# A second folding of the features in a Fourier mixing layer: two half products with 128 contraction rows each, and a later place for the norm transposes

## Chip, core, metric

One core of a Trainium2 chip. TensorE (matmuls, PE in the profile; its weight loads are PEld), VectorE (DVE), ScalarE (ACT), GpSimd (POOL) and the DMA queues run side by side and wait for each other by semaphores. The metric is the device time of one execution in microseconds, lower is better. The kernel before took 360.04 us (median of 3 runs, 356.87 to 361.86).

## What is computed

Block-sparse attention (4 batches, 8 heads, 768 positions, head width 64; each query sees its own 64-wide block and the best three of the earlier ones), then a Fourier mixing layer with a two-layer feed-forward on the 512 joined features:

```python
def _moe_ref(x, w_ch1, w_ch2):
    X = np.fft.fft(x, axis=1)          # over 768 positions
    X = np.fft.fft(X, axis=2)          # over 512 features
    mixed = np.real(X).astype(np.float32)
    u = x + mixed
    mu = np.mean(u, axis=-1, keepdims=True)
    var = np.mean((u - mu) ** 2, axis=-1, keepdims=True)
    un = (u - mu) / np.sqrt(var + 1e-06)
    ch = np.maximum(un @ w_ch1, 0.0) @ w_ch2
    return (u + ch).astype(np.float32)
```

The real part of the double transform is cos·x·cos minus sin·x·sin, so it is made of products with cosine and sine tables. Only the real part of a real input is wanted, so inputs at d and 512 - d (and at s and 768 - s) can be added or subtracted first, and the tables need only half the rows.

## The kernel before

**Attention** runs over 16 head pairs (`kk`, four per batch), each in six steps: scores (`stage_S`, L339) into one of two large PSUM tiles, exponentials on ScalarE (L344), the product with v (`stage_AV`, L365) for the first head at step 4 and for the second at step 1 of the next pair. Around them stand the transposes of q and k of the pair after next (`stage_AA`, `tp`), their evictions (qT on VectorE L259, key sums L265) and the gate that picks the blocks (`stage_B`, `stage_C`).

**Fourier stage.** When a head pair's output x is complete, `stage_AV` makes sums and differences of the two halves of the positions (`fs`, L378 and L379, on GpSimd, for a batch's last pair on VectorE). After pairs 2 and 3 of a batch VectorE folds the features d and 512 - d: differences into `fo` (L385), sums in place in `fs` (L386); the middle column goes to `xmid` (L388, GpSimd). `stage_S1` multiplies over the positions: `za` from `fo` with the sine table and from `xmid`, `ya` from `fs` with the cosine table, for `dt` = 1 and then 0 (two groups of 128 features); VectorE and ScalarE bring the results to SBUF, forwards and backwards (L413, L415). `stage_S2` multiplies over the features: each of the six 128-row tiles `kt` takes four matmuls with 512 columns (L430, L431), contracting 2 x 128 rows of y with cosines and of z with sines, into one PSUM bank `mx`. In batch 0 a fifth matmul with the identity adds x (L434) and ScalarE copies the sum out (L435); in the others VectorE adds x while it empties PSUM (L437). Statistics follow (L439, L440).

**Norm and feed-forward.** After the sixth tile `stage_N` computes 1/std by Newton steps: the start on VectorE (L455 to L458), the steps on GpSimd (L461 to L468), then six normalizations, three on VectorE (L471) and three on ScalarE (L475). `stage_T` transposes the six tiles (`unt`, L484), which are copied to `unT` (L489, in batch 0 L487). `stage_M1` (16 units: 512 and 256 columns, `ha` and `hb`, L500; evictions L503 on ScalarE and L505 on VectorE) and `stage_M2` (24 units of four 512-column matmuls, `ch`, L514; after every fourth the add L517 on VectorE and the output DMA) are the feed-forward.

**Order.** TensorE's and GpSimd's orders are what the program issues; VectorE's and ScalarE's are arranged by the scheduler of the language. A `Feed` holds two lists: `chain`, the Fourier stage of each batch (S1, S2, T, each a `Unit` with a cost, the unit that it follows, and a gap that must pass after that one by the planner's clock), and `bulk`, the M1 and M2 units. Between the attention steps `filler` (L555) pulls units: a ready one of the chain first, then bulk. How many it pulls is set by the work that should be done by step `key`. A batch's M1 and M2 units enter `bulk` after its last T; T of a batch may begin only when M1 of the batch before is done. What is left after attention is pulled in the same manner to the end.

**PSUM.** All stages but the scores share four PSUM buffers (tag `ps`): a tile that is to be written waits until the engine that empties the tile before it in that buffer has done so.

Of the kernel before, what the change touches and what calls it, by code (L numbers as in the profile page):

```python
# [12 lines left out]
F16 = mybir.dt.float16  # L13
# [6 lines left out]
def _consts_np():  # L20
    S = 768
    DM = 512
# [9 lines left out]

    d = np.arange(DM // 2)
    argd = 2.0 * np.pi * ((np.outer(d, np.arange(DM)) % DM) / DM)
    CD = np.cos(argd).astype(np.float16)
    SDN = (-np.sin(argd)).astype(np.float16)
    SDP = np.sin(argd).astype(np.float16)
    SDN[0] = SDP[0] = np.where(np.arange(DM) % 2 == 0, 1.0, -1.0)
    ident32 = np.eye(128, dtype=np.float32)
# [77 lines left out]
def kernel(  # L117
# [40 lines left out]
    def const(shape, dtype, name):  # L158
        return cpool.tile(shape, dtype, tag=name, name=name)

    cs_sb = const([128, HST, 2, KM], F16, "cs_sb")
    ss_sb = const([128, HST, 2, KM], F16, "ss_sb")
    cd_sb = const([128, 2, DM], F16, "cd_sb")
    sdn_sb = const([128, 2, DM], F16, "sdn_sb")
    sdp_sb = const([128, 2, DM], F16, "sdp_sb")
    xmid = const([128, 2, HST, 128], F16, "xmid")
    fs = const([128, 2, HST, DM], F16, "fs")
    fo = const([128, 2, HST, HD], F16, "fo")
    id32 = const([128, 128], FP, "id32")
# [54 lines left out]
    def load_fft():  # L224
        nc.sync.dma_start(cs_sb, dr["CS"].ap().rearrange("(st p) r k -> p st r k", p=128))
        nc.sync.dma_start(ss_sb, dr["SS"].ap().rearrange("(st p) r k -> p st r k", p=128))
        for t, n in ((cd_sb, "CD"), (sdn_sb, "SDN"), (sdp_sb, "SDP")):
            nc.sync.dma_start(t, dr[n].ap().rearrange("(dt p) l -> p dt l", p=128))

# [122 lines left out]
    def stage_AV(kk, e):  # L352
# [26 lines left out]
        eng.tensor_tensor(out=fs[:, 1, :, c], in0=x_b[:, 0:HST, c], in1=x_b[:, HST:NST, c], op=SUB)  # L379
        fsf = fs.rearrange("p r t d -> p (r t) d")  # L380
        fof = fo.rearrange("p r t d -> p (r t) d")
        if hp >= 2:
            lo, hi = (129, HD) if hp == 2 else (1, 129)
            a, z = fsf[:, :, lo:hi], fsf[:, :, DM - lo:DM - hi:-1]
            nc.vector.tensor_tensor(out=fof[:, :, lo:hi], in0=a, in1=z, op=SUB)  # L385
            nc.vector.tensor_tensor(out=a, in0=a, in1=z, op=ADD)  # L386
        if hp == 2:
            nc.gpsimd.tensor_copy(out=xmid.rearrange("p r t d -> p (r t) d")[:, :, 0:1],  # L388
                                  in_=fsf[:, :, HD:HD + 1])


    def stage_S1(b, dt):
        x = X[b]
        dsl = slice(128 * dt, 128 * (dt + 1))
        yps = pst([128, 2, KM], f"ya_{b}_{dt}")
        zps = pst([128, 2, KM], f"za_{b}_{dt}")
        for r in range(2):
            for t in range(HST):
                nc.tensor.matmul(zps[:, r, :], fo[:, r, t, dsl], ss_sb[:, t, r, :],
                                 start=(t == 0), stop=(dt == 1 and t == HST - 1))  # L400
            if dt == 0:
                for t in range(HST):
                    nc.tensor.matmul(zps[:, r, :], xmid[:, r, t, :], cs_sb[:, t, r, :],
                                     start=False, stop=(t == HST - 1))
        for r in range(2):
            for t in range(HST):
                nc.tensor.matmul(yps[:, r, :], fs[:, r, t, dsl], cs_sb[:, t, r, :],
                                 start=(t == 0), stop=(t == HST - 1))
# [10 lines left out]
    def stage_S2(b, kt):  # L419
        x = X[b]  # L420
# [8 lines left out]
        for dt in range(2):  # L429
            nc.tensor.matmul(mps, x["y", dt][hi][:, ksl], cd_sb[:, dt, :], start=(dt == 0), stop=False)  # L430
            nc.tensor.matmul(mps, x["z", dt][hi][:, ksl], sd[:, dt, :], start=False,  # L431
                             stop=(dt == 1 and b > 0))
        if b == 0:
            nc.tensor.matmul(mps, id16, x["x"][:, kt, :], start=False, stop=True)  # L434
            nc.scalar.copy(out=u_b[:, kt, :], in_=mps)  # L435
        else:
            nc.vector.tensor_tensor(out=u_b[:, kt, :], in0=mps, in1=x["x"][:, kt, :], op=ADD)  # L437
        bst = spool.tile([128, 6], FP, tag="bst", name=f"bst_{b}_{kt}")
# [139 lines left out]
    with tc.manual_schedule(engines={mybir.EngineType.PE, mybir.EngineType.Pool}):  # L578
# [124 lines left out]
```

## Time and profile before

| | |
|---|---|
| median of 3 runs | 360.04 us (356.87 to 361.86) |
| the profiled execution | 359.59 us, span 357.6 us, mean granted clock 0.971 |
| end of the last AV on TensorE | 281.6 us |
| first M1 of the last batch | 311.63 us |
| S2 matmuls, 512 columns (L430, L431) | 4 x 24, 378 to 379 ns each, 0.86 us for four in a row |
| add L437 (18) / statistics L439 (24) on VectorE | 676 / 690 ns |
| fold L385, L386 on VectorE | 16 in all, 555 to 570 ns |
| TensorE's waits at `unt` L484 | 4.0 us for L517, 3.1 for qT L259, 1.1 for L471 |

The page gives each engine's busy share; a busy TensorE is a modelled quantity, as matmuls overlap. Slices are a fortieth of the span (8.94 us). The chain of waits follows the end of the program back, at each step to what released the instruction. A group's row gives busy time, mean of one in ns, the idle time of the engine ahead of it and what ended that. The row PEclk, and the granted clock of a window, tell at what share of full speed TensorE was run.

### The profile page before, as it was taken

How to read it: one execution, taken by the hardware profiler on the slowest of the kernel's cores; microseconds unless marked ns; L12 is line 12 of the kernel's file. 1: busy time of each engine (PE TensorE's matmuls, PEld its weight loads, DVE VectorE, ACT ScalarE, POOL GpSimd, SP SyncE). 2: the span in 40 equal slices, each digit the busy share in tenths (PEclk: the TensorE clock that was granted, in tenths of full speed). 3: DMA queues.
4: the chain of work that ended last, by engine and by line, in shares of the span. 5: the costliest groups of instructions: out<-in, count | busy, mean ns of one | idle time of the engine just before them, and what ended most of it. 6: DMA issues, size and time to landing. Idle time of an engine off the chain costs nothing.

```text
span 357.6 us, 6899 instructions
## 1 busy us (share of the span) xinstructions
PE 335.2 (94%) x2688; PEld 212.9 (60%) x2688; DVE 223.0 (62%) x685; ACT 174.2 (49%) x259; POOL 89.1 (25%) x165
## 2 busy tenths in 40 slices
PE   8899997997999999599999999996999999999995
PEld 4577775775766765355566566553766554556442
DVE  3768888777566769755566458787656669533121
ACT  3177885879865744424557444243667320244100
POOL 8434655138440110610402202016012000100000
PEclk9989998999699999999999999998999999999999
DMA  9999999963967322223403210000000010100012
GB/s 180 202 207 251 232 186 212 157 140 88 168 129 119 88 46 75 73 75 103 110 11 73 61 60 29 31 30 32 0 2 2 0 60 29 59 31 0 31 62 85
DMA packets 85696, 31.57 MB, mean 88 GB/s; under 512 B 77736, under 2 KB 81520, under 8 KB 85664
## 3 DMA queue, kind: packets, MB, share of 16 engines
q1 hardware_dynamic: 80368, 26.27, 32.2%
q0 software_dynamic: 3552, 4.40, 7.8%
q10 hardware_dynamic: 1744, 0.46, 0.6%
q8 instruction: 21, 0.34, 0.4%
q14 instruction: 11, 0.09, 0.1%
HBM read 29.03 MB, written 6.29 MB: 99 GB/s over the span
## 4 chain that ended last, share of the span: by engine, by line
PE 74%; DVE 17%; ACT 4%; POOL 3%; issue 2%; POOLq 0%; DVEq 0%; ACTq 0%
PE ch L514 18%; PE ha L500 15%; PE sc L339 8%; PE hb L500 8%; PE g L286 5%; PE av L365 4%; PE tp L254 3%; DVE bst L439 3%; PE warm L318 2%; DVE u L437 2%; PE unt L484 2%; DVE kr L265 2%; PE gt L307 2%; PE mx L430 2%; PE mx L431 2%
## 5 line engine op out<-in xcount | busy, mean ns | idle before, releaser
L344 ACT ACTIVATE ptl<-sc 128x896 f16<-128x896 f32 x96 | 87.4, 916 | 63.6 <-PE sc L339 51.6
L514 PE MATMUL ch<-w_sb,hT 128*128 128x512 f16 x384 | 93.0, 384 | 0.0
L500 PEld LDWEIGHTS <-w_sb 128*128 128x128 f16 x512 | 48.8, 98 | 35.5 <-issue 1.4
L500 PE MATMUL ha<-unT,w_sb 128*128 128x512 f16 x256 | 66.1, 380 | 0.0
L339 PE MATMUL sc<-qg,kI 76*128 76x512 f16 (+3 forms) x256 | 56.6, 314 | 3.9 <-ACT ptl L344 3.9
L514 PEld LDWEIGHTS <-hT 128*128 128x128 f16 x384 | 36.9, 99 | 38.2 <-issue 1.1
L503 ACT ACTIVATE hT<-ha 128x512 f16<-128x512 f32 x64 | 38.2, 597 | 36.3 <-PE ha L500 36.2
L505 DVE TENSOR_SCALAR hT<-hb 128x256 f16<-128x256 f32 x64 | 27.0, 422 | 38.5 <-PE hb L500 38.4
L262 POOL CAST qg<-qT 64x768 f16<-64x768 f32 x32 | 26.7, 835 | 59.2 <-DVE qT L259 57.1
L500 PE MATMUL hb<-unT,w_sb 128*128 128x256 f16 x256 | 38.4, 272 | 0.3 <-DVE hT L505 0.3
L339 PEld LDWEIGHTS <-kI 76*128 76x128 f16 x256 | 24.5, 102 | 20.2 <-issue 3.5
L277 ACT CAST kI<-tp 64x384 f16<-64x384 f32 x57 | 27.0, 473 | 16.6 <-DVE kr L265 15.6
L517 DVE TENSOR_TENSOR u<-ch,u 128x512 f32<-128x512 f32 x24 | 16.5, 687 | 25.2 <-PE ch L514 25.0
L378 POOL TENSOR_TENSOR fs<-x 128x384 f16<-128x384 f16 x12 | 11.6, 970 | 76.4 <-DVE x L370 69.0
L365 PEld LDWEIGHTS <-ptl 128*128 128x128 f16 x672 | 24.7, 98 | 2.9 <-DVE ptl L350 0.4
L365 PE MATMUL av<-v,ptl 128*128 128x65 f16 x672 | 26.2, 195 | 0.1
L265 DVE TENSOR_REDUCE kr<-tp 128x6 f32<-128x384 f32 x32 | 17.0, 548 | 11.0 <-PE tp L254 11.0
L350 DVE TENSOR_TENSOR ptl<-ptl,ut 128x384 f16<-128x384 f16 x36 | 14.2, 430 | 11.5 <-ACT ptl L344 11.4
L286 PEld LDWEIGHTS g<-kr,qT 128*128 128x128 f32 x160 | 20.1, 195 | 1.4
L286 PE MATMUL g<-kr,qT 128*128 128x24 f32 x160 | 19.9, 267 | 0.0
L475 ACT ACTIVATE x<-u,nmr,rstd 128x512 f16<-128x512 f32 x12 | 8.9, 803 | 22.1 <-POOL nmr L468 22.1
L484 PE MATMUL unt<-id,x 128*128 128x128 f16 x96 | 11.0, 247 | 8.3 <-DVE u L517 4.0
(88 smaller groups left out, 423.6 us busy)
## 6 DMA issues: line engine op xcount, KB each, us to landing
vn<-in_v_dram SPq DMA_DIRECT2D x32, 192.0 KB, 4.0
out_dram<-u SPq DMA_DIRECT2D x24, 256.0 KB, 2.0
kn<-in_k_dram SPq DMA_DIRECT2D x30, 192.0 KB, 4.4
qn<-in_q_dram SPq DMA_DIRECT2D x30, 192.0 KB, 4.0
w_sb<-in_moe_w_ch_dram POOLq DMA_DIRECT2D x8, 256.0 KB, 8.1
w_sb<-in_moe_w_ch_dram POOLq DMA_DIRECT2D x4, 512.0 KB, 8.1
cs_sb<-c_CS SPq DMA_DIRECT2D x1, 289.5 KB, 4.7
ss_sb<-c_SS SPq DMA_DIRECT2D x1, 289.5 KB, 4.9
```

Source lines behind the costliest of these rows:

```text
L262: nc.gpsimd.tensor_copy(out=d["qg"][e][0:64, :], in_=d["qt"][64 * e:64 * e + 64, :])
L265: nc.vector.tensor_reduce(out=d["kr12"][:, 6 * g:6 * g + 6], in_=ps.rearrange("p a (x c) -> p a x c", x=2), axis=mybir.AxisListType.X, op=ADD)
L277: nc.scalar.copy(out=dst, in_=src_)
L286: nc.tensor.matmul(gps[:, st - 1, :], d["qt"][:, 128 * st:128 * (st + 1)], d["kr24"], start=True, stop=True)
L339: nc.tensor.matmul(sp[:, co:co + (a1 - a0)], d["kI"][e][0:76, 128 * jt:128 * (jt + 1)], d["qg"][e][0:76, a0:a1], start=True, stop=not diag)
L344: nc.scalar.activation(out=pt[:, SEC * s:SEC * (s + 1)], in_=sp[:, 0:SEC], func=AF.Exp, scale=0.125)
L365: nc.tensor.matmul(av[:, st, 0:65], pt[:, o:o + 128], d["v16"][:, e, jt, 0:65], start=(cnt == 0), stop=(cnt == 20))
L484: nc.tensor.transpose(tps[:, dt, :], x["x"][:, st, 128 * dt:128 * (dt + 1)], id16)
L500: nc.tensor.matmul(hp_, w1_sb[:, dt, 128 * it:128 * (it + 1)], unT[:, dt, c0:c1], start=(dt == 0), stop=(dt == NDT - 1))
L503: nc.scalar.activation(out=hT[:, c0:c1], in_=hp_, func=AF.Relu)
L505: nc.vector.tensor_scalar(out=hT[:, c0:c1], in0=hp_, scalar1=0.0, scalar2=None, op0=mybir.AluOpType.max)
L514: nc.tensor.matmul(cps, x["hT"][it][:, 128 * st:128 * (st + 1)], w2_sb[:, it, :], start=(it == 0), stop=(it == NIT - 1))
```

## The change

`stage_AV`: the folded sums and differences are folded once more, d against 256 - d. Features of the even output columns l = 2m need only the sums (cosine) or differences (sine) of one kind, those of the odd columns the other kind. So `fc[0]` and `fo[0]` (128 features) serve the even columns, `fc[1]` and `fo[1]` the odd ones. After pair 2 two VectorE operations make `ft[0]` and `ft[1]` from features around 256; after pair 3 six make `ft[2]`, `ft[3]`, `fo[1]`, `fc[1]`, `fo[0]`, `fc[0]`, and GpSimd does the columns at 0, 128, 256 and 384 (two small operations after each of the two pairs). `fs` is no longer written in place.

`stage_S1` reads `fo[dt]` and `fc[dt]`; its matmuls have the shapes of before. `stage_S2`: for each `dt` two matmuls with 256 columns write their half of the PSUM tile, even columns in the first half and odd ones in the second. What reads the tile takes the two halves alternately (`mv`), and the identity matmul of batch 0 reads x with the columns reordered. The tables CD, SDN and SDP have half as many rows.

In the planner the cost of an S2 unit goes from 0.87 to 0.5 and the gap after it from 0.7 to 1.0; the gap ahead of the first T goes from 5.0 to 9.0 except in batch 0; `key` goes from 12 x 12 + 20 to 12 x 12 + 29.

```diff
-    d = np.arange(DM // 2)
-    argd = 2.0 * np.pi * ((np.outer(d, np.arange(DM)) % DM) / DM)
+    d = np.arange(DM // 4)
+    l = 2 * np.arange(DM // 2)[None, :] + np.arange(2)[:, None]
+    argd = 2.0 * np.pi * ((d[:, None, None] * l[None]) % DM) / DM
...
-    cd_sb = const([128, 2, DM], F16, "cd_sb")
+    cd_sb = const([128, 2, HD], F16, "cd_sb")
...
-    fo = const([128, 2, HST, HD], F16, "fo")
+    fc = [const([128, 2 * HST, 128], F16, f"fc_{p}") for p in range(2)]
+    fo = [const([128, 2 * HST, 128], F16, f"fo_{p}") for p in range(2)]
+    ft = [const([128, 2 * HST, 128], F16, f"ft_{i}") for i in range(4)]
...
-        if hp >= 2:
-            lo, hi = (129, HD) if hp == 2 else (1, 129)
-            a, z = fsf[:, :, lo:hi], fsf[:, :, DM - lo:DM - hi:-1]
-            nc.vector.tensor_tensor(out=fof[:, :, lo:hi], in0=a, in1=z, op=SUB)
-            nc.vector.tensor_tensor(out=a, in0=a, in1=z, op=ADD)
         if hp == 2:
-            nc.gpsimd.tensor_copy(out=xmid.rearrange("p r t d -> p (r t) d")[:, :, 0:1],
-                                  in_=fsf[:, :, HD:HD + 1])
+            near, far = f[:, :, HD - 1:HD - 128:-1], f[:, :, HD + 1:HD + 128]
+            tt(ft[0][:, :, r], near, far, SUB)
+            tt(ft[1][:, :, r], near, far, ADD)
+            for p, op in ((0, ADD), (1, SUB)):
+                tt(fc[p][:, :, 0:1], f[:, :, 0:1], f[:, :, HD:HD + 1], op, nc.gpsimd)
+        if hp == 3:
+            near, far = f[:, :, r], f[:, :, DM - 1:DM - 128:-1]
+            tt(ft[2][:, :, r], near, far, SUB)
+            tt(fo[1][:, :, r], ft[2][:, :, r], ft[0][:, :, r], ADD)
+            tt(fo[1][:, :, 0:1], f[:, :, 128:129], f[:, :, 384:385], SUB, nc.gpsimd)
+            tt(xmid.rearrange("p r t d -> p (r t) d")[:, :, 0:1], f[:, :, 128:129],
+               f[:, :, 384:385], ADD, nc.gpsimd)
+            tt(ft[3][:, :, r], near, far, ADD)
+            tt(fc[1][:, :, r], ft[3][:, :, r], ft[1][:, :, r], SUB)
+            tt(fo[0][:, :, r], ft[2][:, :, r], ft[0][:, :, r], SUB)
+            tt(fc[0][:, :, r], ft[3][:, :, r], ft[1][:, :, r], ADD)
...
         for dt in range(2):
-            nc.tensor.matmul(mps, x["y", dt][hi][:, ksl], cd_sb[:, dt, :], start=(dt == 0), stop=False)
-            nc.tensor.matmul(mps, x["z", dt][hi][:, ksl], sd[:, dt, :], start=False,
+            half = mps[:, HD * dt:HD * (dt + 1)]
+            nc.tensor.matmul(half, x["y", dt][hi][:, ksl], cd_sb[:, dt, :], start=(dt == 0), stop=False)
+            nc.tensor.matmul(half, x["z", dt][hi][:, ksl], sd[:, dt, :], start=False,
                              stop=(dt == 1 and b > 0))
+        split = dict(m=HD, r=2)
+        xv = x["x"][:, kt, :].rearrange("p (m r) -> p m r", **split)
+        uv = u_b[:, kt, :].rearrange("p (m r) -> p m r", **split)
+        mv = mps.rearrange("p (r m) -> p m r", **split)
         if b == 0:
-            nc.tensor.matmul(mps, id16, x["x"][:, kt, :], start=False, stop=True)
-            nc.scalar.copy(out=u_b[:, kt, :], in_=mps)
+            nc.tensor.matmul(mps, id16, xv.rearrange("p m r -> p r m"), start=False, stop=True)
+            nc.scalar.copy(out=uv, in_=mv)
         else:
-            nc.vector.tensor_tensor(out=u_b[:, kt, :], in0=mps, in1=x["x"][:, kt, :], op=ADD)
+            nc.vector.tensor_tensor(out=uv, in0=mv, in1=xv, op=ADD)
...
-    M1_COST, M2_COST, S1_COST, S2_COST, T_COST = 1.3, 0.87, 1.3, 0.87, 0.43
+    M1_COST, M2_COST, S1_COST, S2_COST, T_COST = 1.3, 0.87, 1.3, 0.5, 0.43
...
-            last = Unit(lambda kt=kt: stage_S2(b, kt), S2_COST, last, 2.5 if kt == 0 else 0.7)
+            last = Unit(lambda kt=kt: stage_S2(b, kt), S2_COST, last, 2.5 if kt == 0 else 1.0)
...
-            last = Unit(lambda st=st: stage_T(b, st), T_COST, last, 5.0 if st == 0 else 0.2,
+            last = Unit(lambda st=st: stage_T(b, st), T_COST, last, (5.0 if b == 0 else 9.0) if st == 0 else 0.2,
...
-        key = 12 * (3 * NP) + 20
+        key = 12 * (3 * NP) + 29
```

More of the change, by code (lines that the diff above doesn't have):

```diff
@@ L30, in _consts_np @@
     SS = np.sin(arg).astype(np.float16)
-    d = np.arange(DM // 2)
-    argd = 2.0 * np.pi * ((np.outer(d, np.arange(DM)) % DM) / DM)
+    d = np.arange(DM // 4)
+    l = 2 * np.arange(DM // 2)[None, :] + np.arange(2)[:, None]
+    argd = 2.0 * np.pi * ((d[:, None, None] * l[None]) % DM) / DM
     CD = np.cos(argd).astype(np.float16)
-    SDN = (-np.sin(argd)).astype(np.float16)
-    SDP = np.sin(argd).astype(np.float16)
-    SDN[0] = SDP[0] = np.where(np.arange(DM) % 2 == 0, 1.0, -1.0)
+    sn = np.sin(argd)
+    sn[0] = np.sin(np.pi * l / 2)
+    SDN, SDP = (-sn).astype(np.float16), sn.astype(np.float16)
+    SDN[0, 0] = SDP[0, 0] = np.where(np.arange(DM // 2) % 2 == 0, 1.0, -1.0)
     ident32 = np.eye(128, dtype=np.float32)
@@ L162 @@
     ss_sb = const([128, HST, 2, KM], F16, "ss_sb")
-    cd_sb = const([128, 2, DM], F16, "cd_sb")
-    sdn_sb = const([128, 2, DM], F16, "sdn_sb")
-    sdp_sb = const([128, 2, DM], F16, "sdp_sb")
+    cd_sb = const([128, 2, HD], F16, "cd_sb")
+    sdn_sb = const([128, 2, HD], F16, "sdn_sb")
+    sdp_sb = const([128, 2, HD], F16, "sdp_sb")
     xmid = const([128, 2, HST, 128], F16, "xmid")
     fs = const([128, 2, HST, DM], F16, "fs")
-    fo = const([128, 2, HST, HD], F16, "fo")
+    fc = [const([128, 2 * HST, 128], F16, f"fc_{p}") for p in range(2)]
+    fo = [const([128, 2 * HST, 128], F16, f"fo_{p}") for p in range(2)]
+    ft = [const([128, 2 * HST, 128], F16, f"ft_{i}") for i in range(4)]
     id32 = const([128, 128], FP, "id32")
@@ L227, in load_fft @@
         for t, n in ((cd_sb, "CD"), (sdn_sb, "SDN"), (sdp_sb, "SDP")):
-            nc.sync.dma_start(t, dr[n].ap().rearrange("(dt p) l -> p dt l", p=128))
+            nc.sync.dma_start(t, dr[n].ap())
     def load_w1(part):
@@ L379, in stage_AV, with tt @@
         eng.tensor_tensor(out=fs[:, 1, :, c], in0=x_b[:, 0:HST, c], in1=x_b[:, HST:NST, c], op=SUB)
-        fsf = fs.rearrange("p r t d -> p (r t) d")
-        fof = fo.rearrange("p r t d -> p (r t) d")
-        if hp >= 2:
-            lo, hi = (129, HD) if hp == 2 else (1, 129)
-            a, z = fsf[:, :, lo:hi], fsf[:, :, DM - lo:DM - hi:-1]
-            nc.vector.tensor_tensor(out=fof[:, :, lo:hi], in0=a, in1=z, op=SUB)
-            nc.vector.tensor_tensor(out=a, in0=a, in1=z, op=ADD)
-        if hp == 2:
-            nc.gpsimd.tensor_copy(out=xmid.rearrange("p r t d -> p (r t) d")[:, :, 0:1],
-                                  in_=fsf[:, :, HD:HD + 1])
+        f = fs.rearrange("p r t d -> p (r t) d")
+        r = slice(1, 128)
+        def tt(out_, a, b_, op, eng=nc.vector):
+            eng.tensor_tensor(out=out_, in0=a, in1=b_, op=op)
+        if hp == 2:
+            near, far = f[:, :, HD - 1:HD - 128:-1], f[:, :, HD + 1:HD + 128]
[14 more added lines that the diff above has]
+            tt(fc[0][:, :, r], ft[3][:, :, r], ft[1][:, :, r], ADD)
     def stage_S1(b, dt):
         x = X[b]
-        dsl = slice(128 * dt, 128 * (dt + 1))
         yps = pst([128, 2, KM], f"ya_{b}_{dt}")
@@ L398, in stage_S1 @@
             for t in range(HST):
-                nc.tensor.matmul(zps[:, r, :], fo[:, r, t, dsl], ss_sb[:, t, r, :],
+                nc.tensor.matmul(zps[:, r, :], fo[dt][:, HST * r + t, :], ss_sb[:, t, r, :],
                                  start=(t == 0), stop=(dt == 1 and t == HST - 1))
@@ L406, in stage_S1 @@
             for t in range(HST):
-                nc.tensor.matmul(yps[:, r, :], fs[:, r, t, dsl], cs_sb[:, t, r, :],
+                nc.tensor.matmul(yps[:, r, :], fc[dt][:, HST * r + t, :], cs_sb[:, t, r, :],
                                  start=(t == 0), stop=(t == HST - 1))
@@ L604 @@
         nc.gpsimd.memset(xmid, 0.0)
-        nc.gpsimd.memset(fo[:, :, :, 0:1], 0.0)
+        nc.gpsimd.memset(fo[0][:, :, 0:1], 0.0)
         stage_W(11)
```

## The prediction

> **What bounds it now.** I read the page first (busy shares, slices, chain of waits), then groups by shape, then windows and timeline where TensorE stands still.
>
> ```profile
> PE 335.2 (94%) x2688; PEld 212.9 (60%) x2688; DVE 223.0 (62%) x685; ACT 174.2 (49%) x259; POOL 89.1 (25%) x165
> PE   8899997997999999599999999996999999999995
> DVE  3768888777566769755566458787656669533121
> PEclk9989998999699999999999999998999999999999
> PE 74%; DVE 17%; ACT 4%; POOL 3%; issue 2%; POOLq 0%; DVEq 0%; ACTq 0%
> ```
>
> TensorE fills nearly every slice and 74% of the chain. The holes are slice 17 (143 to 152 us) and slice 28 (241 to 250); VectorE stands at 8 or 9 tenths just before slice 17. So there are two limits: TensorE nearly everywhere, VectorE's queue around each batch's Fourier stage. The groups by shape give the prices:
>
> ```profile
> L500 PE MATMUL hb<-unT,w_sb 128*128 128x256 f16 x256 | 38.4, 272 | 0.3 <-DVE hT L505 0.3
> L430 PE MATMUL mx<-cd_sb,yT 128*128 128x512 f16 x24 | 9.1, 379 | 0.0
> L437 DVE TENSOR_TENSOR u<-mx,x 128x512 f32<-128x512 f32 x18 | 12.2, 676 | 2.2 <-PE mx L431 1.9
> L439 DVE BATCH_NORM_STATS2 bst<-u 128x6 f32<-128x512 f32 x24 | 16.6, 690 | 1.9 <-ACT u L435 1.3
> L386 DVE TENSOR_TENSOR fs<-fs 128x762 f16<-128x762 f16 x4 | 2.2, 556 | 0.1
> ```
>
> A matmul's mean includes its drain; the timeline gives the spacing. Four 512-column matmuls start 0.86 us apart as a group, four 256-column ones 0.43. The hole of batch 1, and granted clock by window (third column TensorE busy, PEclk after the counts):
>
> ```profile
> 146.40 2.05 DVE L471 TENSOR_SCALAR x<-u,stat,rstd 128x512 f16<-128x512 f32 x3 [1.31 <-POOL rstd L466]
> ...
> 149.35 0.68 DVE L517 TENSOR_TENSOR u<-ch,u 128x512 f32<-128x512 f32 x1
> ...
> 150.09 0.38 PE L484 MATMUL unt<-id,x 128*128 128x128 f16 x4 [3.97 <-DVE u L517]
> ```
> ```profile
> 85.51:88.93 3.42, 1.79 (x18) 1.47 (x18) 2.50 (x6) 3.42 (x6) 3.30 (x5) 1.00 0.00 1
> 88.93:95.75 6.82, 6.82 (x53) 5.61 (x53) 3.55 (x19) 6.32 (x12) 1.89 (x4) 0.50 0.87 142
> 143.40:146.80 3.40, 2.71 (x16) 1.46 (x14) 1.32 (x6) 0.92 (x1) 2.17 (x11) 1.00 0.09 22
> 146.80:150.20 3.40, 0.11 (x3) 0.21 (x4) 3.40 (x6) 2.23 (x3) 2.42 (x3) 1.00 0.42 94
> 150.20:153.65 3.45, 3.45 (x19) 1.84 (x17) 1.51 (x4) 0.92 (x1) 2.46 (x3) 0.52 0.20 76
> ```
>
> The transpose waited not for its data (147.0) but for a PSUM buffer: four buffers serve nearly all stages, VectorE empties most of them in queue order, and the add L517 that frees this one stood behind three normalizations that waited for POOL. A standstill also has a second price: after a window of 3.4 us with 1.79 us or less of TensorE work the clock is 0.50 for the next; after 2.71 it stays 1.00. A halved window costs 1.7 us of matmul work.
>
> **The change, part by part.** Its end is priced against the profiled execution's 359.59 us (span 357.6 and 2.0 around it), 0.45 below the median 360.04.
>
> *Half products.* 24 tiles x 4 matmuls go from 512 to 256 columns: 0.86 - 0.43 = 0.43 us a tile, 2.6 a batch, 10.3 in all, if nothing else ends later. Weight loads (97 ns median in L431) hide under 108 ns, as they do in hb. The identity matmul of batch 0 now steps over every second element: six times between 0.216 and 0.43 us, nothing to 1.3; I take 0: za's 193 columns show 0.083 us each whatever they read, and the step is two elements only.
>
> *Fold.* After the last head pair two VectorE operations become six, four times 0.57 = 2.3 us, and in the built program they stand ahead of evictions that TensorE needs. POOL's four 6-element operations (0.2 to 0.6 us, as L388) run beside them; the casts behind them on POOL wait for qT longer anyway. Batch by batch:
> - Batch 0: za waited for fo at 58.12. Now two sums and a copy (0.57, 0.57, 0.48) go before it: 59.8, so 1.7 later.
> - Batch 1: from the end of the last AV (118.84) ya came 3.98 us later. Its buffer is now that of hb 12, emptied behind the whole fold: 1.74 + 6 x 0.58 + two mask products 0.62 + 0.42 = 6.15. Wait 2.2.
> - Batch 2: ya takes the first q transpose's buffer, emptied at 6.6 by the same sum with the copy 0.55 in place of 0.42; TensorE is there at 4.6. Wait 2.0, where 0.25 was.
> - Batch 3: M2 work (4.3 us) covers the fold, but za 0 waits 0.6 for the add that now stands behind it.
>
> *Faster halves before a queue that isn't faster.* A tile costs VectorE 0.68 + 0.69 + 0.18 = 1.55 us as before. From the first half product of batch 1, VectorE's queue in the built order holds six tiles 9.3, reciprocals and AV outputs 1.6, gate work 1.6, key sums 1.45, four masks 1.4, one hT 0.4, one M2 add 0.7, q copies 1.1, Newton start 0.5: 18 us without a break. Against TensorE's groups (M2 0.86, scores 0.38, M1 1.30, gate 1.03, transposes 0.66): the third tile's add ends at 7.35 where its buffer is asked for at 6.8, the fourth's at 10.2 against 9.05; then, behind Newton's 2.35 on POOL, an M2 add at 23.5 against 23.05 and the gate copies at 24.5 against 23.8. Waits 0.55 + 1.15 + 0.5 + 0.7 = 2.9. Batch 2 the same way: 8.35 against 7.65, and an M2 buffer behind an add at 11.25 against 9.15: 2.8.
>
> *Transposes later.* From the last half product to the first transpose there are now 10.1 us of TensorE work in batch 1 (batch 2: 10.0) against the 9.3 that VectorE's queue took. That removes 0.31 + 3.97 + 1.7 of clock = 6.0 us in batch 1, and 0.25 + 0.49 + 1.25 + 2.17 + 1.7 = 5.9 in batch 2. What is late next is in the paragraph above. Batch 0's gap stays at 5.
>
> *The last batch.* There the later plan has no cover left. All M2 work goes between and after the halves (two groups a tile), and then six transposes stand alone. From the end of the last AV: M2 4.3, the first products 2.5 and the wait of 0.6, M2 2.6, five tiles with 0.43 + 1.73, the last 0.43, small gaps 0.1: last half product at 21.4. On VectorE then add, statistics and Newton start to 23.7, an L517 add to 24.4, rstd 2.35 after the second Newton step (26.95), normalizations 1.46 for three, another L517 add to 29.1, four copies of 0.42: M1 starts at 30.85. Before it was 311.63 - 281.6 = 30.0. So the 2.6 us of the halves are lost and 0.85 more. TensorE's work ended at 26.6, six transposes of 0.24 aside: some 2.8 us of standstill, so the clock halves as M1 begins: 0.85 to 1.7, I take 1.3.
>
> *Key 20 to 29* spreads filler; at the end of attention the same M2 work is left in both built programs (20 + 76 matmuls), so nothing by itself. The constant tables halve (three DMAs of 256 KB): the start waits for no DMA of theirs, 0.
>
> Sum: batch 0: -2.6 + 1.7 + 0.9 (clock held down one window longer, half chance of 1.7) = 0.0. Batch 1: -2.6 - 6.0 + 2.2 + 2.9 + 0.85 (the same half chance) = -2.65. Batch 2: -2.6 - 5.9 + 2.0 + 2.8 + 0.85 = -2.85. Batch 3: +0.85 + 1.3 = +2.1. Together -3.4: 356.2, as a median 356.6; I say 357. Ends: without any new clock loss and with all of batch 0's gain -9 (350.6); with every one, and normalizations at 0.69 as in the other batches, +2 (361.6).
>
> **A rule against a row.** The row: windows with 1.75 us (54.8 to 58.2) and 1.79 us of work were followed by half clock. The Trainium skill, "TensorE: Matmul & The Clock Gate" (its table of the two states), asks for an idle window of about 3.4 us, and advises against gaps over 3 us. By that rule none of my four charges for the clock (0.9 + 0.85 + 0.85 + 1.3) would fall and the sum would be 3.9 us lower; the trace decides, and it charges them.
>
> **An unseen price.** The add L437 (and batch 0's copy) now reads PSUM alternating between two halves 1 KB apart. No row does that. Nearest is L415, which reads the same kind of tile backwards in 572 ns for 384 elements, where a forward cast (L275) takes 559. So I take 0.68 as before; no gain is possible as the element count is the same. Upper end: its streaming part, (676 - 282) / 392 = 1.0 ns an element from L289 with 120, doubles: 1.2 us. The skill's "Vector Engine (DVE) Microarchitecture Reference", section 5.2, speaks against the change here: a source that hops every element took 1.73 against 1.05 ns a column (measured there in SBUF); by it each add would be 0.35 us longer and the sum about 5 us higher.
>
> **Rivals.**
> 1. *TensorE stays the only bound.* The buffer waits do not show because VectorE starts each stage with slack. For it: before, all waits of TensorE for the products' buffers were 0.8 us. Against: VectorE already stood full from 134 to 143 us. Then batches 0 to 2 give 2.6 + 8.6 + 8.5 and the tail +0.85: 341; half of it lies at 349.
> 2. *The interleaved read is slow.* Place: 18 adds in VectorE's full stretches. At 1.2 us each, 12 x 0.52 = 6.2 in batches 1 and 2, and in batch 3 VectorE needs 2.47 us a tile against 2.16 of TensorE, five times 0.3 and the last add 0.5, 2.1: 357 + 8.3 = 365. From 0.15 us an add upward it turns the gain into a loss. For it: nothing in the trace; against: the backward read.
> 3. *The products do not get shorter* (weight loads bind): hb's 0.43 speaks against it; the waits stay, and TensorE comes later to them: 358 to 360.
>
> **How the numbers follow.** About 2% (7.2 us) is what a measurement of this kernel tells from no change; its three runs spread over 1.4%. Forecast 0.53 (351 to 362), rival 1 0.20 (at or under 352 in most of it), rival 2 0.24, rival 3 0.03. Under 352.8: 0.18 of rival 1 and 0.04 of the forecast's low end, 0.22. Over 367.2: rival 2 with clock losses besides, 0.16. The range 349.5 to 366 leaves out the lower part of rival 1 and the upper of rival 2.
>
> **What would show it.** Halves 0.43 us a tile; no wait for L517 at batch 1's first transpose; waits of about 2 us at ya in batches 1 and 2; M1 of the last batch about 31 us after the last AV with half clock; L437 at 0.68. Wrong if VectorE's stretch is broken by idle time, or L437 is above 0.8.

## The result and the profile after

The changed kernel took **346.13 us** (median of 4 runs, 345.73 to 346.31) beside 358.46 (4 runs, 355.66 to 361.86) for the kernel before: ratio 0.968, 95% interval 0.960 to 0.976, so 3.2% faster. The prediction added up to -3.4, said 357 and gave 349.5 to 366. The sign was right, the size was not: 12.3 us came where 3.4 were forecast. The profiled execution took 346.12 us with a span of 344.3; that of before 359.59 with 357.6. Line numbers from here on are those of the kernel that a row comes from; the changed kernel's are 5 to 22 higher than those of before for the same operation.

Page of the changed kernel: busy shares, slices (a fortieth of the span, 8.6 us), chain of waits.

```profile
PE 320.4 (93%) x2688; PEld 210.2 (61%) x2688; DVE 229.1 (67%) x701; ACT 172.7 (50%) x259; POOL 93.5 (27%) x177
PE   7899994998899989999999989899999999899995
DVE  2788889788565779887566688986544868533211
PEclk9999998799699999999999999999999999999999
PE 74%; DVE 12%; ACT 4%; POOL 4%; issue 3%; DMA 2%; ACTq 0%; POOLq 0%; DVEq 0%
```

The two holes of before (slices 17 and 28) are gone; from slice 13 on the clock stays full. One hole is new, in slice 7 of batch 0. The parts of the change, in the groups by shape:

```profile
L448 PE MATMUL mx<-cd_sb,yT 128*128 128x256 f16 x24 | 5.9, 272 | 0.0
L456 PE MATMUL mx<-x,id 128*128 128x512 f16 x6 | 2.3, 389 | 0.0
L459 DVE TENSOR_TENSOR u<-mx,x 128x512 f32<-128x512 f32 x18 | 12.2, 680 | 1.4 <-PE mx L449 1.3
L389 DVE TENSOR_TENSOR ft<-fs 128x762 f16<-128x762 f16 x16 | 9.4, 629 | 2.5 <-POOL fs L384 2.4
L389 DVE TENSOR_TENSOR fo<-ft,ft 128x762 f16<-128x762 f16 x8 | 5.0, 625 | 0.0
```

Four half products in a row start 0.11 us apart, 0.43 a tile, as forecast. The add that reads the two PSUM halves alternately takes 680 ns (676 before), the identity matmul 389 (379): both free. The two groups of fold operations shown average 0.63 instead of 0.55 (the third, `fc`, stays at 0.55), and three operations of batch 0 make all of that (1.08, 1.17 and 1.17 us, experiment 4). What TensorE waits for in the changed kernel (total, times, longest):

```profile
PE za L416 <- POOL dummyp L227: 4.5, 1, 4.5
...
PE ya L424 <- DVE hT L527: 1.4, 1, 1.4
PE ch L536 <- DVE u L539: 1.2, 1, 1.2
...
PE ya L424 <- DVE qT L264: 1.1, 1, 1.1
...
PE mx L448 <- DVE u L459: 0.4, 1, 0.4
```

(For za the wait ended with fo at 60.41 us; the GpSimd instruction named there ended a moment later and has no part in za.) The predicted waits at ya are there, 1.4 and 1.1 us where 2.2 and 2.0 were forecast; of the 5.7 us at the products and behind them 0.4 and 1.2 came.

**An account by stretches.** All comparisons below cut the profiled execution at events that every kernel has: the first AV on TensorE, the first M1 of batch 0, the start of the last group of AV matmuls, the first M1 of the last batch. In windows of 0.5 us, a stretch's length less TensorE's busy time is *standstill*; busy time times one less the granted clock is what *half clock* cost; the rest is *work* at full clock. In us:

| kernel | batch 0: work, standstill, clock | batches 1 and 2: work, standstill, clock | last batch: work, standstill, clock | sum |
|---|---|---|---|---|
| before | 59.35, 6.5, 4.7 | 173.5, 8.7, 3.75 | 30.55, 0.1, 0 | 287.2 |
| after | 56.85, 10.2, 5.0 | 168.7, 4.5, 0 | 28.7, 1.3, 0 | 275.1 |
| difference | -2.5, +3.7, +0.3 | -4.8, -4.3, -3.75 | -1.9, +1.2, 0 | -12.0 |

Another 0.96 us lies ahead of the first AV: in some profiles (before among them, after not) a stretch at 17 to 20 us ran at half clock, with one and the same code; that is left out of what follows. The half clock in the table is that of one execution each, and a program's executions differ in it (last section), by 1.7 us for one window of 3.4 us more or less: the mean granted clock of the kernel before is 0.971 in the execution shown and 0.965 to 0.990 in the others. The last batch's work and standstill repeat within 0.02 us in the twelve kernels that share the changed kernel's order there. Shorter products bring 9.2 us of work. Batch 0 and the last batch give back about half of it as standstill, and the two middle batches lose 8 us of standstill and half clock on top. So the question for the experiments: what removed those 8 us, and what took the rest of the halves.

### The profile page after: what moved, and what is told of

It reads as the page before. It is cut to its first block, busy times and chain, and to the rows that moved or that the text cites. A ratio compares the mean times of both kernels' runs of the same rounds, so it can differ in the third digit from the quotient of the medians.

```text
span 344.3 us, 6929 instructions
## 1 busy us (share of the span) xinstructions
PE 320.4 (93%) x2688; PEld 210.2 (61%) x2688; DVE 229.1 (67%) x701; ACT 172.7 (50%) x259; POOL 93.5 (27%) x177
## 4 chain that ended last, share of the span: by engine, by line
PE 74%; DVE 12%; ACT 4%; POOL 4%; issue 3%; DMA 2%; ACTq 0%; POOLq 0%; DVEq 0%
PE ch L536 21%; PE ha L522 15%; PE hb L522 8%; PE sc L344 8%; PE g L291 5%; PE av L370 5%; PE tp L259 3%; ACT kI L282 2%; DVE kr L270 2%; DVE mx L301 2%; DMA qn<-in_q_dram 2%; PE gt L312 1%; PE ya L424 1%; PE mx L448 1%; DVE bst L461 1%
## 5 line engine op out<-in xcount | busy, mean ns | idle before, releaser
L536 PE MATMUL ch<-w_sb,hT 128*128 128x512 f16 x384 | 91.2, 379 | 1.3 <-DVE u L539 1.2
L344 PE MATMUL sc<-qg,kI 76*128 76x512 f16 (+3 forms) x256 | 55.7, 309 | 4.1 <-ACT ptl L349 4.0
L536 PEld LDWEIGHTS <-hT 128*128 128x128 f16 x384 | 36.1, 97 | 36.8 <-issue 1.4
L539 DVE TENSOR_TENSOR u<-ch,u 128x512 f32<-128x512 f32 x24 | 16.5, 688 | 21.6 <-PE ch L536 21.3
L291 PE MATMUL g<-kr,qT 128*128 128x24 f32 x160 | 20.6, 271 | 0.0
L348 PE MATMUL sc<-ltri,id 128*128 128x128 f16 x84 | 18.6, 222 | 0.0
L375 DVE TENSOR_TENSOR x<-av,rcp 128x384 f16<-128x384 f32 x32 | 17.8, 557 | 1.0
```

Of the source, the lines that this page charges most:

```text
L291: nc.tensor.matmul(gps[:, st - 1, :], d["qt"][:, 128 * st:128 * (st + 1)], d["kr24"], start=True, stop=True)
L344: nc.tensor.matmul(sp[:, co:co + (a1 - a0)], d["kI"][e][0:76, 128 * jt:128 * (jt + 1)], d["qg"][e][0:76, a0:a1], start=True, stop=not diag)
L348: nc.tensor.matmul(sp[:, co:co + 128], id16, ltri, start=False, stop=True)
L536: nc.tensor.matmul(cps, x["hT"][it][:, 128 * st:128 * (st + 1)], w2_sb[:, it, :], start=(it == 0), stop=(it == NIT - 1))
```

## Experiments

Each ratio is against the kernel before in runs on the same chip (its medians there: 358.0 to 358.6).

**1. The plan alone, the products alone.**

```diff
-            last = Unit(lambda st=st: stage_T(b, st), T_COST, last, 5.0 if st == 0 else 0.2,
+            last = Unit(lambda st=st: stage_T(b, st), T_COST, last, (5.0 if b == 0 else 9.0) if st == 0 else 0.2,
...
-        key = 12 * (3 * NP) + 20
+        key = 12 * (3 * NP) + 29
```

> The kernel before with only the later transposes (gap 9.0 in batches 1 to 3) and key 12*12+29; fold and products as before. Theory A (most of the gain is the standstill at the norm transposes and the halved clock behind it): the waits at unt of 4.0 and 2.2 us and the two windows at half clock (1.7 us each) go, 9 to 11 us less, ratio 0.970 to 0.975. Theory B (the gain is the shorter products; the transposes were only one wait among others that move elsewhere): 3 us or less, ratio 0.99 to 1.0. By the prediction on record, which put 6.0 + 5.9 us on this part with the products' queue unchanged: ratio 0.967 to 0.975 as well, but with 2 to 3 us lost in the last batch.

347.36 us (346.26 to 348.19), ratio 0.967 (0.960 to 0.974). With the old products and fold the plan gives nearly the whole gain; the changed kernel's own ratio, 0.968, can't be told from it. Theory A fits. The reverse, products and fold with the old plan:

> The changed kernel with the old plan for the transposes (gap 5.0 everywhere, key 12*12+20); half products and second fold stay. Theory A: the transposes again stand for VectorE's queue in batches 1 and 2 (3 to 5 us each, with half clock behind it in some), so the time is within 4 us of before, ratio 0.985 to 1.0. Theory B: 8 us or more faster than before, ratio 0.975 or less.

353.35 us, ratio 0.983 (0.975 to 0.990): 4.8 us, somewhat more than theory A allowed and short of the 8 that B asked for. So 10.8 and 4.8 separately, and 12.3 together.

**2. Which half of the plan?** The gap on the kernel before, then the key.

> The kernel before with the gap ahead of the transposes at 9.0 in batches 1 to 3 and nothing else (key stays 12*12+20, products and fold as before). It splits the plan alone (ratio 0.967) into its two edits. Theory A (the standstill at the transposes and the halved clock behind it are the gain): ratio 0.965 to 0.972, as with both. Rival K (key is a part of it, as it moves feed-forward work from ahead of the last third to later steps): at least 3 us of the 10.8 are missing, ratio 0.975 or more.

357.39 us, ratio 0.997 (0.994 to 1.001). Nothing: theory A falls as it stood, and rival K named 3 us where all were missing. The list of waits of this kernel shows why a later place alone doesn't help:

```profile
PE av L365 <- DVE qT L259: 2.0, 1, 2.0
PE gt L307 <- DVE u L517: 1.9, 1, 1.9
```

None of the 4.0 us at unt is left; the same VectorE operations (qT, the add L517) are now waited for by the attention instructions that took the transposes' old place. Batches 1 and 2 cost 6.7 us of standstill and 6.8 of half clock (before: 8.7 and 3.75); the profiled execution, 359.81 us, is the slowest of ten (mean granted clock 0.967, the others 0.967 to 0.983), so a typical one has less half clock.

> The kernel before with key 12*12+29 and nothing else (gap 5.0, products and fold as before). The gap alone gave 0.997, gap and key together 0.967. Theory I (the two work only together: the later transposes need feed-forward work that is still left then, and at key 20 it is used up; in the built program of the gap alone no M2 matmul is left between the transposes of batch 2, with key 29 there are 16): key alone leaves the waits for VectorE's queue at the transposes, ratio 0.985 to 0.997. Theory K (key alone is the lever, transposes starved of filler in either place): ratio 0.965 to 0.975.

350.71 us, ratio 0.979 (0.973 to 0.986), between both theories. With the old products the key is the larger part: standstill in batches 1 and 2 falls from 8.7 to 3.6 and half clock from 3.75 to 0.3; the gap then brings it to 1.3 and 0. How the key takes the wait of batch 1 away is only partly seen: the first transpose waits there 0.8 us for qT instead of 4.0 for L517, and other attention steps stand beside it. That was not taken apart further.

The same two numbers taken back in the changed kernel, one at a time:

```diff
-        key = 12 * (3 * NP) + 29
+        key = 12 * (3 * NP) + 20
```

> The changed kernel with key back at 12*12+20 (gap 9.0, half products and fold stay). Theory I: batch 2 again has no M2 matmul left between its transposes (20 ahead of them, none between), so half clock and waits come back there: 350 to 354 us. Theory G (with the shorter products the gap suffices): 346 to 348 us.

```diff
-            last = Unit(lambda st=st: stage_T(b, st), T_COST, last, (5.0 if b == 0 else 9.0) if st == 0 else 0.2,
+            last = Unit(lambda st=st: stage_T(b, st), T_COST, last, 5.0 if st == 0 else 0.2,
```

> The changed kernel with the gap back at 5.0 (key 12*12+29, half products and fold stay). Theory I: 16 and 20 M2 matmuls (3.4 and 4.3 us) and scores 5 times between the last half product and the first transpose, against some 9 us that VectorE and GpSimd need for it, so 3 to 4 us of waits in each of the two batches: 350 to 354 us. Theory K: 346 to 348 us.

352.63 us (ratio 0.982, 0.973 to 0.990) and 352.77 (0.985, 0.979 to 0.991): with half products each number without the other is worth hardly anything over having neither (353.35; 0.6 to 0.7 us, within the spread), and both together 7.2 us. Theory I holds in both, and the traces show two different causes. With key 20, TensorE around the transposes of batch 2 (start, length, and in brackets the wait):

```profile
235.55 0.55 PE L344 MATMUL sc<-qg,kI 76*128 76x512 f16 x3
237.37 0.80 PE L370 MATMUL av<-v,ptl 128*128 128x65 f16 x21 [1.27 <-DVE qT L264]
238.55 0.91 PE L344 MATMUL sc<-qg,kI 76*128 76x512 f16 x2 [0.38 <-ACT ptl L349]
239.25 0.63 PE L506 MATMUL unt<-id,x 128*128 128x128 f16 x4
239.68 2.27 PE L291 MATMUL g<-kr,qT 128*128 128x24 f32 x10
```

No `ch` from 234.68 us on: the M2 work is used up, nothing fills, and the windows of the same kernel (TensorE's busy time is the second number, the granted clock the third from the end; cut where the clock changes) show half clock behind it:

```profile
235.18:238.58 3.40, 1.75 (x31) 1.26 (x31) 3.37 (x7) 3.10 (x5) 3.17 (x4) 1.00 0.02 5
238.58:241.98 3.40, 3.40 (x19) 2.96 (x19) 2.42 (x7) 1.64 (x2) 1.74 (x3) 0.50 0.22 80
```

With gap 5.0 there is M2 work, but the transposes stand in front of it in TensorE's order and wait for the normalization, in batch 1:

```profile
145.26 0.46 PE L312 MATMUL gt<-id,gmp 128*44 128x128 f16 x5
147.94 0.40 PE L506 MATMUL unt<-id,x 128*128 128x128 f16 x4 [2.22 <-DVE x L493]
148.17 1.13 PE L536 MATMUL ch<-w_sb,hT 128*128 128x512 f16 x4
```

The program's own order tells the same beforehand. M2 matmuls of batches 1 and 2 from the last half product to the first transpose / between the transposes:

| | batch 1 | batch 2 |
|---|---|---|
| before | 16 / 12 | 16 / 4 |
| gap alone | 32 / 20 | 20 / 0 |
| key alone | 20 / 16 | 16 / 12 |
| plan alone (gap and key) | 32 / 12 | 32 / 16 |
| after, key 20 | 32 / 12 | 20 / 0 |
| after, gap 5.0 | 16 / 16 | 20 / 16 |
| after | 32 / 16 | 32 / 16 |

Is it the length of the cover, or a lucky place? The changed kernel with 7.0:

> The changed kernel with the gap ahead of the transposes at 7.0 in batches 1 to 3 (5.0 gave 352.8 us, 9.0 gives 346.1). Theory I: by the lengths in the trace some 7.4 us of TensorE's work then lie between the last half product and the first transpose, against 8.9 us that the statistics, the Newton steps and the normalizations took: 1.5 us of wait in each of the two batches and in one of them perhaps half clock, 348.5 to 351 us. Rival (the place among the attention steps decides, not the length): 346 or 353 us.

348.89 us (348.05 to 349.53; ratio 0.975, 0.972 to 0.978): 5.0, 7.0, 9.0 give 352.8, 348.9, 346.1. It is gradual, as the length theory says (the rival named 346 or 353); in batch 1 a wait of 1.6 us for L539 appears at the AV beside the transposes, and no half clock in batches 1 and 2.

**3. What the second fold costs.** Its four VectorE operations a batch are left out (and with them a part of what is computed); the position products read `ft`:

```diff
-            tt(fo[1][:, :, r], ft[2][:, :, r], ft[0][:, :, r], ADD)
...
-            tt(fc[0][:, :, r], ft[3][:, :, r], ft[1][:, :, r], ADD)
...
-                nc.tensor.matmul(zps[:, r, :], fo[dt][:, HST * r + t, :], ss_sb[:, t, r, :],
+                nc.tensor.matmul(zps[:, r, :], (ft[2] if dt == 1 else ft[0])[:, HST * r + t, :], ss_sb[:, t, r, :],
...
```

> The changed kernel without the four second-fold operations on VectorE (fo and fc left out, the position product reads ft directly, so the combination of near and far features is left out of what is computed); all matmuls keep their shapes and order. It prices the fold. The prediction on record: the fold costs 1.7 us in batch 0, 2.2 in batch 1 (ya), 2.0 less 0.25 in batch 2 and 0.6 in batch 3, so 6 us faster than the changed kernel. Theory C (the fold costs what the trace of the changed kernel shows: 2 us in batch 0 where it runs beside GpSimd's casts, 1.0 to 1.4 us at ya in batches 1 and 2, nothing in the last): 4 us faster, 341 to 343 us.

342.21 us (341.04 to 342.62), 3.9 less than the changed kernel: theory C. By stretches it is 2.4 in batch 0, 2.7 in batches 1 and 2, nothing in the last. Against the plan alone (same plan, long products) this kernel shows what the halves are worth with no fold to pay: 6.45 us by the account (1.2, 4.0 and 1.3 in the three stretches) of 9.4 us less work. What is missing is mostly standstill, in each stretch (0.9, 0.75, 0.9). That fits a norm chain on VectorE and GpSimd that doesn't get shorter with the products; no run tests it by itself.

**4. Batch 0's fold beside GpSimd.** VectorE in the changed kernel and, in the next fence, GpSimd at the same time:

```profile
57.14 2.18 DVE L389 TENSOR_TENSOR ft<-fs 128x762 f16<-128x762 f16 x2
59.24 1.17 DVE L389 TENSOR_TENSOR fo<-ft,ft 128x762 f16<-128x762 f16 x1
60.33 0.55 DVE L389 TENSOR_TENSOR fc<-ft,ft 128x762 f16<-128x762 f16 x1
```

```profile
56.98 1.92 POOL L267 CAST qg<-qT 64x768 f16<-64x768 f32 x2
58.97 1.03 POOL L224 CAST v<-vn 128x768 f16<-128x768 f32 x1
```

Three operations take twice their time while GpSimd casts, the next one doesn't. The casts began 0.16 us ahead of the fold (56.98 against 57.14 us). One instruction makes GpSimd wait for the fold:

```diff
                 for e in range(2):
+                    if kk == 6 and e == 0: nc.gpsimd.tensor_copy(out=dummyp[0:1, 0:1], in_=fc[0][0:1, 0, 5:6])
                     nc.gpsimd.tensor_copy(out=d["qg"][e][0:64, :],
```

> The changed kernel with one more instruction on GpSimd: before the casts of qT of pair 6 it copies one element of fc[0], so that these casts and the v cast behind them run after batch 0's fold instead of beside it. Theory D (a VectorE operation of two f16 sources takes 1.17 instead of 0.55 us while GpSimd casts): the three long fold operations of batch 0 take 0.55 us each, za of batch 0 starts 1.8 to 2.4 us earlier and its wait of 4.5 us falls to about 2.5, 344 us. Rival (the fold operations are long for another reason, such as waiting for their small GpSimd columns): durations stay at 1.17 and the time stays at 346.

```profile
56.68 1.03 DVE L390 TENSOR_TENSOR ft<-fs 128x762 f16<-128x762 f16 x2
57.63 0.55 DVE L390 TENSOR_TENSOR fo<-ft,ft 128x762 f16<-128x762 f16 x1
```

Durations as theory D has them (the timeline of that kernel above: two in 1.03, then 0.55), and the wait at za falls from 4.5 to 2.8. The time is 345.01 us (343.83 to 346.79), 1.1 less by the medians and 2.0 by the account; the intervals overlap (0.954 to 0.970, and 0.960 to 0.976), so the durations are shown, the gain in time is likely and not measured sharply.

**5. Half clock in batch 0.** On top of experiment 4's kernel, 14 matmuls ahead of za, into za's own buffer:

```diff
         zps = pst([128, 2, KM], f"za_{b}_{dt}")
+        for _ in range(14 if b == 0 and dt == 1 else 0):
+            nc.tensor.matmul(zps.rearrange("p r m -> p (r m)"), warm[:, 0:128], warm[:, 0:KH], start=True, stop=True)
```

> The changed kernel with GpSimd's casts of pair 6 behind batch 0's fold, and with 14 matmuls of 386 columns into the za buffer of batch 0 ahead of the real ones (their result is overwritten), 2.3 us of work in a wait of 2.8 us. Theory E (the half clock in batch 0 follows from the windows of 3.4 us in which TensorE stood still for the fold): no window at half clock between 56 and 64 us, 1.5 to 2 us faster than with the casts later alone (345.0), 343 us. Rival: the clock halves all the same, or ScalarE and VectorE set the pace of batch 0 at full clock too: 345 us.

343.49 us (342.93 to 344.31), ratio 0.959 (0.957 to 0.961). Windows of the changed kernel, and of this one:

```profile
53.40:56.80 3.40, 1.85 (x17) 0.98 (x15) 3.31 (x10) 3.36 (x5) 0.13 (x1) 1.00 0.99 194
56.80:60.20 3.40, 0.00 (x0) 0.00 (x0) 3.37 (x4) 0.16 (x1) 3.28 (x6) 0.53 1.08 228
60.20:63.60 3.40, 3.05 (x33) 2.94 (x34) 3.16 (x7) 0.91 (x2) 2.37 (x5) 0.50 0.91 148
```

```profile
51.14:54.54 3.40, 2.51 (x36) 1.79 (x35) 3.24 (x10) 2.63 (x6) 0.09 (x1) 1.00 1.08 232
54.54:57.94 3.40, 3.40 (x27) 2.21 (x28) 3.31 (x10) 2.58 (x3) 0.39 (x2) 1.00 0.72 160
57.94:61.34 3.40, 2.89 (x44) 2.34 (x43) 3.34 (x8) 1.05 (x2) 0.98 (x3) 1.00 1.23 231
...
78.34:81.74 3.40, 2.23 (x20) 1.49 (x20) 2.28 (x10) 2.26 (x4) 2.22 (x11) 1.00 0.97 217
81.74:85.14 3.40, 2.59 (x30) 2.10 (x31) 3.29 (x7) 3.39 (x5) 3.34 (x4) 0.50 0.45 88
```

In the first, 1.85 and then 0 us of work, and two windows at half clock; in the second no window under 2.5 us around the fold, and none: theory E. The last two rows are ahead of batch 0's transposes: 2.23 us of work and half clock behind it, one window more there than in the changed kernel, so the account shows 1.05 us of the 1.5 and in batch 0 as a whole no less half clock (4.7 us, 4.5 in experiment 4's kernel); in the kernels of experiments 7 to 9, with the same batch 0, it is 3.25 to 3.4. So the clock around the fold is shown, the gain in time, again, is likely (the runs of the two kernels overlap). With gap 8.0 for batch 0 too:

> As the run with the 14 matmuls, and in batch 0 too the transposes come later (gap 8.0 instead of 5.0). Theory A carried over: in batch 0 the transposes at 84 us stand for x (0.3), for a buffer behind qT (0.9) and the scores behind them for ScalarE (0.8), then 6.8 us at half clock; later transposes find all ready: 3 to 4 us faster than with gap 5.0. Rival: batch 0 has no feed-forward work to fill with, attention alone runs at ScalarE's pace, and feed-forward starts later: no change or up to 2 us slower.

346.70 us, 3.2 slower, and the rival was too mild. Scores now wait 2.8 us in one place for ScalarE's exponentials, and batch 0's stretch is 2.8 us longer: without feed-forward work to fill, a later transpose only starts that work later.

**6. How near is VectorE's queue?** Statistics computed twice in batches 1 and 2:

```diff
-        nc.vector.bn_stats(out=bst, in_=u_b[:, kt, :])
+        for _ in range(2 if b in (1, 2) else 1): nc.vector.bn_stats(out=bst, in_=u_b[:, kt, :])
```

> The changed kernel with the statistics of each product tile computed twice in batches 1 and 2 (12 more VectorE operations of 0.69 us, 0.60 apart). It asks how close VectorE's queue is to the path. The prediction on record (the queue holds 18 us without a break and sets the waits for buffers): nearly all of 12 x 0.60 = 7.2 us is added, 351.5 to 353.5 us. Theory Q (in the changed kernel the queue of batch 1 runs 16.0 us, is idle again from 145.2 us, and the first transpose comes 1.3 us after the last normalization): the first 1 to 2 us of each batch are hidden, 2 to 4 us in all are added, 348 to 350 us.

351.33 us (351.08 to 352.41): 5.2 more. Theory Q missed, and the prediction's reading (351.5 to 353.5) was nearly met; by the medians it is 72% of 7.2, in batches 1 and 2 alone 4.6. So the prediction was right that the queue is near the path. It was wrong on how long the queue is.

**7. The waits at ya.** S1 gap 5.5 instead of 3.5 in batches 1 and 2, on top of experiment 5:

> The version with the later casts and the 14 matmuls (343.5 us), with the gap ahead of the first S1 unit at 5.5 instead of 3.5 in batches 1 and 2. Theory F (the waits of 1.4 and 1.1 us at ya are the second fold in VectorE's queue ahead of the eviction that frees ya's buffer, and lie on the path): with the stage later by about 2 us of other TensorE work the waits go, 2 to 2.5 us faster, 341 to 341.5 us. Rival: the stage meets other waits at its new place, no gain or up to 3 us slower.

344.39 us against 343.49: no gain. The waits at ya are gone, others have come:

```profile
PE mx L451 <- DVE u L462: 1.5, 2, 1.3
...
PE mx L451 <- ACT kI L283: 1.0, 1, 1.0
...
PE unt L509 <- DVE kr L276: 0.8, 1, 0.8
```

**8. The last batch.** There the gap after a product tile 0.3 instead of 1.0, so that one M2 group goes between two tiles and 44 M2 matmuls (24 before) stay to cover the norm:

```diff
-            last = Unit(lambda kt=kt: stage_S2(b, kt), S2_COST, last, 2.5 if kt == 0 else 1.0)
+            last = Unit(lambda kt=kt: stage_S2(b, kt), S2_COST, last, 2.5 if kt == 0 else (0.3 if b == 3 else 1.0))
```

> As the run with the S1 gap of 5.5, and in the last batch the gap after each product tile 0.3 instead of 1.0 (one M2 group between two tiles instead of two; 44 M2 matmuls instead of 24 stay to cover the norm). Theory H (in the last batch 1.3 us of standstill is left, by the norm that starts late): 0.5 to 1 us less than without, no more, as all other time there is TensorE's work. The prediction on record, which saw 2.6 + 0.85 us lost there: 2.5 to 3.5 us less.

> The version with the later casts and the 14 matmuls (343.5 us) with the last batch's gap of 0.3 alone. Theory H: 342.5 to 343 us. The prediction on record: 340 to 341 us.

With it experiment 7's kernel takes 342.79, and experiment 5's **341.65 us** (341.51 to 342.12), ratio 0.955 (0.952 to 0.957), the fastest of the study: by the medians 1.6 and 1.8 us less, between theory H and the prediction's reading. From the start of the last group of AV matmuls to M1 both traces show 28.75 us where 30.0 were: 1.25, a little over theory H. Standstill there is down to 0.4 us, so hardly more is to be had from cover.

**9. A still later key,** 36 on experiment 5's kernel:

> The version with the later casts and the 14 matmuls (343.5 us) with key at 12*12+36. Theory I: key 29 already leaves 16 M2 matmuls between the transposes, there is nothing more to gain: 343 to 344.5 us; beyond it M2 work that the end must take grows only if the last batch gets more, and the built program leaves it the same. Theory K (later is better without end): under 342 us.

345.83 us, 2.3 slower than with 29; both theories missed. Batches 1 and 2 hold 5.75 us of standstill against 4.3: the wait of 1.2 us at ch is gone, and 1.2 at M1's hb and 0.8 at a transpose have come.

## Why the prediction failed, by its own steps

- **Half products (-10.3).** Right: 0.43 a tile, 9.2 us less work in the account. Identity matmul and interleaved read at nothing: right (rival 2 is out; by its own price, 8.3 us at 0.52 an add, it would have turned the gain into a loss from about 0.2 us an add and not from 0.15). The surcharge of 0.35 us an add, an estimate from the two figures that the Trainium skill's "Vector Engine (DVE) Microarchitecture Reference" (section 5.2) has for SBUF, did not show on PSUM: 680 against 676 ns.
- **Fold.** Batch 1 and 2: 2.2 and 2.0 forecast, 1.4 and 1.1 measured, same buffers, same culprit (the forecast's sum for batch 1 gives 6.26 as written, not 6.15, and that for batch 2 6.4, not 6.6). Batch 0: za 1.7 later forecast; it took 2.8 us longer from the first AV than in the plan alone (37.0 against 34.2), as three operations doubled beside GpSimd. The forecast had GpSimd's casts wait for qT; qT was done at 56.06 us, and they began at 56.98, behind GpSimd's two small operations and just ahead of the fold. Last batch: 0.6 forecast, none. All together some 4 us (experiment 3).
- **"Faster halves before a queue that isn't faster" (2.9 + 2.8): the step that failed.** VectorE's 18 us were a sum of durations, and the sum was right: the rows from 129.15 to 145.19 us add up to 18.2. But they took 16.0 us. In the trace a VectorE operation starts before the one ahead has ended, here in the changed kernel:

```profile
129.85 0.68 DVE L459 TENSOR_TENSOR u<-mx,x 128x512 f32<-128x512 f32 x1
130.57 0.69 DVE L461 BATCH_NORM_STATS2 bst<-u 128x6 f32<-128x512 f32 x1
131.18 0.34 DVE L355 TENSOR_TENSOR ptl<-ptl,ut 128x384 f16<-128x384 f16 x1
131.44 0.18 DVE L462 BATCH_NORM_AGGREGATE stat<-bst 128x2 f32<-128x6 f32 x1
131.53 0.33 DVE L355 TENSOR_TENSOR ptl<-ptl,ut 128x384 f16<-128x384 f16 x1
```

  Starts are 0.61, 0.26 and 0.09 us apart where durations are 0.69, 0.34 and 0.18; a dependent pair (the add and, straight behind it, its statistics) keeps its full 0.72. Of the 40 rows 32 begin before the one ahead has ended, 2.55 us together, against 0.34 us of idle time: 18.25 - 2.55 + 0.34 = 16.04. TensorE asked when it was forecast to, or a little earlier; it was VectorE that was ready sooner. Counted from the first half product of batch 1 (128.95 us), the third tile's add ended at 6.65 (forecast 7.35) and the product that was due at 6.8 began at 6.79 without a wait; the fourth's ended at 8.97 (10.2), asked for at 8.64 (9.05): a wait of 0.4 where 1.15 was forecast. In batch 2, from 209.73 us, the M2 buffer came free at 9.8 (11.25) and was asked for at 8.6 (9.15): 1.2 where 2.1 was forecast. So of 5.7 us 1.6 came, and of the other four on the list, 0.5 to 0.7 us each, none. Experiment 6 says the same from the other side: VectorE work added to this queue is paid at 72%. The prediction's own rows of before held the overlap (statistics 0.69 long, next start 0.60 later).
- **Transposes later (-6.0, -5.9).** Right in size: no wait at unt and no half clock in batches 1 and 2. The reason given was half of it. **"Key 20 to 29 ... nothing by itself"** was wrong: it compared the M2 work left at the end of attention, and what counts is the M2 work left at the transposes of batch 2. In the changed kernel the key is worth 6.5 us, and the gap nothing clear without it.
- **The last batch (+2.1).** -0.7 instead. Counted as the forecast counted, from the start of the last AV matmul (281.6 us in the kernel before, where its end is at 281.8), the last half product was done at 20.7 us (21.4 forecast) and M1 began at 29.4 (30.85): six copies went 0.34 us apart, not 0.42, normalizations and adds overlapped in the same way, and no half clock, as the standstill was 1.3 us and not 2.8.
- **Four charges for the clock (3.9).** Batch 0's came in another place and size (+0.3 net), the other three not at all. The row behind them was no accident: windows with 1.75 us of work (key 20) and 1.85 (after, batch 0) were followed by half clock. It was the standstills that were not there. The rule of the Trainium skill's "TensorE: Matmul & The Clock Gate" (its table of the two states), which asks for an idle window of about 3.4 us, would have given the better total, but these windows, about half busy, contradict it. The prediction's own limit (half clock after 1.79 us of work or less) is no sharp one either: with gap 7.0 a window of 1.79 us was followed by full clock (last section).
- **Sum.** For batches 1 and 2: work -5.2 forecast, -4.8 measured; standstill +1.5 against -4.3; clock -1.7 against -3.75. Batch 0: 0 against +1.5. Last: +2.1 against -0.7. Rival 1 (341, VectorE with slack) was nearer in number than the forecast (346.1 came); its reason does not hold, as experiment 6 found little slack and the fold's waits came.

## What to carry to other kernels

Line up a queue by the starts in a timeline, not by the sum of durations; where waits are decided by half a microsecond, overlap of 0.09 us an operation turns them. When a planner moves a step later, count what is left to fill with at that point in every batch, in the built order: a longer gap without stock moves the waits to the neighbours, and here, with half products, two edits that looked like a main one and a by-product were worth 7.2 us together and nothing clear apart (with the old products the by-product alone was worth 7.8 of 10.8). An edit that shortens one engine's work pays only where a chain on the other engines isn't the limit; here two thirds of it.

## Of the hardware, not expected

- A VectorE operation with two f16 sources in SBUF took 1.08 to 1.17 us instead of 0.55 when it started while a GpSimd cast was running (the changed kernel: casts from 56.98, 57.86 and 58.97 us, fold operations from 57.14, 58.14 and 59.24). When it started first, it kept its time and the cast was the longer one: in the kernel before L385 at 57.51 and L386 at 58.61 took 0.56 and 0.57, and the casts that began at 57.65 and 58.79 took 1.08 and 1.06 instead of 0.82. With key 20 the fold operation at 58.86 kept 0.54, and the cast of v at 59.09 took 0.99. So in these rows the one that started second paid. The Trainium skill's "GPSIMD Engine Reference" (section 8) names this contention: GpSimd shares its SBUF interfaces with VectorE and contends with VectorE instructions that have two SBUF inputs.
- TensorE's clock changed on a grid: half clock came in stretches of 3.41 us or two or three of them, and its starts in one trace lie whole multiples apart (57.00 and 87.72 us in the changed kernel: nine). With windows cut on that grid, from 20 us on, every window at full clock with less than 1.79 us of TensorE work in it was followed by half clock in all 18 traces, and none with more than 2.62. Between the two, both happened: 2.24 (experiment 5, at 78.30 us) and 2.62 (the plan alone, 86.78) were followed by half clock, 1.79 (gap 7.0, 146.65) and 2.16 (the changed kernel, 217.43) were not. So the work in the window alone doesn't decide there, and what does stays open. The grid lies elsewhere in each execution, so one and the same program can lose a window more or less.
